# An attention-and-MLP kernel on one core: seven pairs instead of six on the seven-product path in the second group of tokens

## The chip, the core and the metric

The kernel runs on one core of a Trainium2 chip, as one launch. The metric is device time in microseconds, from one execution's start to its end. Before the change the median of three runs is 631.63 us (631.11 to 635.12).

TensorE (PE in the profile) multiplies matrices, with its weight loads shown apart as PEld. VectorE (DVE), ScalarE (ACT) and GpSimd (POOL) work elementwise. SyncE (SP) issues most of the transfers; ACT's queue issues some too.

## The reference

```
scores = scale * q @ k.T                      # 4 batches, 8 heads, 768 tokens, head size 64
keep   = is_global | is_local                 # 8 global keys, 96 local ones
scores = where(keep, scores + bias, -1e9)     # bias = -slope[head] * distance
a      = softmax(scores)
x      = (a @ v) as 3072 tokens x 512
h      = x @ w_in                             # 512 x 2048
out    = maximum(0.01 * h, h) @ w_out         # 2048 x 512
```

The weights come as float64, the rest as float32. The kernel keeps the accuracy by splitting every factor of the MLP into a high part and a low remainder and adding three products for each: high by high, low by high, high by low.

## The kernel before

The 3072 tokens go through as eleven groups: two of 384 tokens, then nine of 256. Attention is worked out one event ahead of the MLP that needs it: `late_event(t)` multiplies the attention weights of event t-2 with v (L360) and the queries and keys of event t (L218) into one PSUM tile `ps_av`, of which there is a single buffer; then come the bias and the row minima on DVE (L232), four exponentials on ACT (L245), the reciprocals (L266, L267) and four scalings on ACT (L274). `turn` transposes 32x32 blocks on DVE (L292) and sends the result through DRAM and back (`via` L256, then four `pt_d` L258), for use two events later.

The change is in the nine groups of 256 tokens. They are one loop over 72 **slots** (L902), eight for each group; slots 0 to 7 are the first group, 8 to 15 the second, 16 to 23 the third. A slot s handles one **pair** p of hidden blocks (256 of the 2048 hidden columns):

- `hidden_pair(s)` (L556): 24 matmuls of 128x256 on PE into `ps_h` (even slots) or `ps_p` (odd slots), one buffer each. The second half of their weights comes from `ring`, two buffers that are filled by transfers from DRAM (L544), issued in ACT's queue two slots ahead.
- `gates(s)`: ACT copies the sums out of PSUM (L567); DVE applies the gate (L569), and on the seven-product path four more sums of activation blocks (L572); ACT rounds to the high part `gh` (L578); DVE takes the remainder `gl` (L581).
- `products(s-2)` (L612): the second matmuls of the pair of two slots before, into banks that collect a whole group (`ps_m`, `ps_q`).

So PE's order in a slot is: an event of attention if one falls there, `hidden_pair(s)`, `products(s-2)`. This order is written out and fixed. Each engine runs its own instructions strictly in order. On DVE and ACT the order within this loop is decided when the program is built, by a scheduler; it may put an instruction well ahead of the slot in whose `gates` call it was written.

A pair goes one of two ways in `products`. The plain way is 12 matmuls of 128x512. The seven-product way forms a 2x2 block product with seven block products instead of eight: 21 matmuls of 128x256 (for pair 7, which comes first, two of them are 128x512). It needs `gates` to make the four sums of activation blocks, so `gh` and `gl` are 896 wide rather than 512, and it needs four **sums of weight blocks** for each pair, (p, 0) to (p, 3), which are made once and stay. Each, in `prepare` (L720), is three additions on DVE (L592) into one of two work buffers `wk`, a rounding on ACT (L737) and one subtraction on DVE (L592). Sums 0, 1 and 2 go to the tiles `h7`/`l7` to `h1`/`l1`; sum 3 goes over a block of the weights `wout` itself. So (p, 3) waits until the last plain pair p has been multiplied.

`SEVEN` (L33) says how many pairs of each group take the seven-product way: 0 in the first group, 6 in the second, 7 in the other seven groups. `order_of` (L526) puts the plain pairs first and the others after them from 7 downward. `sums_at` (L898 to L901) says in which slot's `gates` call each weight sum is written.

After a group's last products, `results` copies the banks out: `part<-ps_m` on ACT (L700), and, after a group of plain pairs alone, `part<-ps_q` on DVE (L702). These banks are written again two slots into the next group: the first group's last products run in slot 9, its banks are copied out, and slot 10 begins with `products(8)` in the same banks.

Of the kernel before, what the change touches and what calls it, by code (L numbers as in the profile page):

```python
# [29 lines left out]
CHUNKS = [3] * 2 + [2] * 9  # L30
STD = 2
PAIR = 2
SEVEN = [0, 6] + [7] * 7  # L33
RING = 2
EDGE = 8
LEAD_CONV = 7
# [17 lines left out]
def fast_path(ctx, tc, qp, kp, vp, wi, wo, nvec, convert, nmall, out, B, H, S):  # L54
# [11 lines left out]
    NP = NF // 2  # L66
# [59 lines left out]
    def pin(ins):  # L126

        if pinned[0]:
            tc.keep_in_program_order(ins)
# [396 lines left out]
    def order_of(c):  # L526

        n = SEVEN[c - STD]
        return list(range(NP - n)) + list(range(NP - 1, NP - 1 - n, -1))
# [57 lines left out]
    def fast(c, p):  # L587

        return p >= NP - SEVEN[c - STD]

# [105 lines left out]
    def results(c):  # L696
# [3 lines left out]
        pin(nc.scalar.copy(out=rows[0], in_=bank[3]))  # L700
        if not SEVEN[c - STD]:
            pin(nc.vector.tensor_copy(out=rows[1], in_=bank[4]))  # L702
# [66 lines left out]
    for j in range(len(order)):  # L769
# [117 lines left out]
        if j == LEFT + NF:  # L887
            early.close()
            for name, n in (("pt", 2), ("t", 2)):
# [6 lines left out]
    bank.append(ps_s.tile([P, 2 * GT], F32, tag="ps_q", name="ps_q"))  # L896
    three = [(p, n) for p in (7, 6, 5, 4) for n in range(3)]
    sums_at = {2 + n: three[2 * n:2 * n + 2] for n in range(6)}  # L898
    sums_at.update({NP: [(3, 0), (3, 1)], NP + 1: [(6, 3)], NP + 2: [(7, 3), (3, 2)], NP + 3: [(5, 3), (2, 0)],
                    NP + 4: [(4, 3), (2, 1)], NP + 5: [(3, 3), (2, 2)], NP + 6: [(2, 3)]})  # L900
    sums_at.update({2 * NP + 4 + n: [(1, n)] for n in range(4)})  # L901
    for s in range(NS):  # L902
        pinned[0] = s == 0
        for t in ev_pair.get(s, ()):
# [280 lines left out]
def tile_kernel(tc, a, out, B, H, S):  # L1185
    nc = tc.nc
    NF, _, NK, _ = a["wi"].shape
    DM = a["wo"].shape[3]
    NB = S // P
    with tc.tile_pool(name="keep", bufs=1) as keep, tc.tile_pool(name="xs", bufs=1, space=bass.MemoryType.DRAM) as dram:  # L1190
        nvec, convert = read_counts(tc, keep, a["ngl"])
        nmall = keep.tile([P, B * NB * H], F32, name="nmall")
        flag = fast_path(tc, a["qp"], a["kp"], a["vp"], a["wi"], a["wo"], nvec, convert, nmall, out, B, H, S)
        with tc.If(flag == 0):
            xs = dram.tile([B, S // 256, P, NK, 256], F32, name="xs")
            general_attention(tc, a["qt"], a["kt"], a["vt"], nvec, xs, B, H, S)
            general_ffn(tc, a["wi"], a["wo"], xs, out)
# [50 lines left out]
```

## Time and profile before

| What | Value |
|---|---|
| median of three runs | 631.63 us |
| the profiled execution | 631.47 us, of which its span 629.6 us |
| around the span | 1.9 us |
| PE busy | 607.6 us (97%) |
| DVE busy | 458.2 us (73%) |
| ACT busy | 345.9 us (55%) |
| mean granted TensorE clock | 0.996 |

The page gives the share of each engine over the whole span and in 40 slices. The chain of work that ended last is followed back from the last instruction to whatever released it. The timeline lists an engine's instructions with start, duration and, in brackets, how long the engine stood idle before and what ended the wait. The windows view gives the busy time of every engine in chosen stretches.

In this execution the second group's slots lie as follows on PE (start of the attention event or, without one, of `hidden_pair`): slot 8 at 237.25, slot 9 at 244.41, slot 10 at 251.58, slot 11 at 257.07, slot 12 at 264.02, slot 13 at 269.47, slot 14 at 276.06, slot 15 at 281.36 and slot 16 at 286.48 us. Attention events fall into slots 8, 9, 11, 13, 16, 17, 19 and 21.

### The profile page before, as it was taken

To read this page: it belongs to the slowest core of one execution; us is meant where nothing else is said; L and a number is where in the kernel's file an instruction comes from. 1 tells how busy PE (TensorE), PEld (TensorE's weight loads), DVE (VectorE), ACT (ScalarE), POOL (GpSimd) and SP (SyncE) were. 2 spreads that over 40 slices of the span, in tenths; PEclk is the share of its full clock that TensorE was granted. 3 is DMA by queue.
4 is the path that set the end of the run, shared out by engine and by line. 5 is a ranking of instruction groups with operands and counts; after the bars stand their busy time and mean duration, and the time that the engine had idled before them with its cause. 6 is when DMAs were issued, how large, how long until landed. Compare 5 with 4: busy or idle time off the path is not lost.

```text
span 629.6 us, 16801 instructions
## 1 busy us (share of the span) xinstructions
PE 607.6 (97%) x6555; PEld 561.6 (89%) x6555; DVE 458.2 (73%) x1312; ACT 345.9 (55%) x901; POOL 68.3 (11%) x118
## 2 busy tenths in 40 slices
PE   5689999999999999999999999999999999999996
PEld 4578899988888898999999999999999999999996
DVE  6989879995456997966975765766766765845654
ACT  6987755554435556556556655654655665532321
POOL 3212200000101001111011101101100100110000
PEclk9899999999999999999999999999999999999999
DMA  8886545623447755865765775855875774733411
GB/s 272 306 295 212 194 144 191 201 101 120 152 158 231 252 180 172 248 201 189 240 226 170 261 224 173 253 181 160 266 238 159 247 223 153 231 104 101 135 68 40
DMA packets 63336, 120.72 MB, mean 192 GB/s; under 512 B 8976, under 2 KB 28432, under 8 KB 63248
## 3 DMA queue, kind: packets, MB, share of 16 engines
q1 hardware_dynamic: 52880, 82.34, 40.8%
q10 hardware_dynamic: 10368, 37.23, 17.9%
q8 instruction: 53, 0.87, 0.6%
q14 instruction: 35, 0.29, 0.2%
HBM read 96.21 MB, written 23.33 MB: 190 GB/s over the span
## 4 chain that ended last, share of the span: by engine, by line
PE 85%; DVE 7%; DMA 3%; ACT 2%; issue 1%; SPq 1%; DVEq 0%; ACTq 0%
PE ps_m L612 22%; PE ps_p L556 16%; PE ps_h L556 15%; PE ps_h L472 9%; PE ps_q L612 6%; PE ps_av L360 5%; PE ps_av L218 4%; PE ps_o L1180 3%; PE ps_o L1181 3%; PE ps_o L1182 3%; DMA via<-pr 1%; DMA pt_d<-via 1%; ACT pr L245 1%; DVE w L949 1%; DVE pr L232 1%
## 5 line engine op out<-in xcount | busy, mean ns | idle before, releaser
L578 ACT CAST gh<-t 128x896 fp32r<-128x896 f32 (+1 forms) x73 | 62.5, 858 | 100.9 <-DVE t L572 56.7
L581 DVE TENSOR_TENSOR gl<-t,gh 128x896 fp32r<-128x896 f32 (+1 forms) x73 | 71.5, 980 | 49.7 <-ACT gh L578 49.7
L245 ACT ACTIVATE pr<-pr,nmall 128x192 f32<-128x192 f32 (+1 forms) x192 | 83.3, 436 | 24.0 <-DVE nmall L232 23.4
L612 PE MATMUL ps_m<-wout,gh 128*128 128x256 f32 (+1 forms) x398 | 85.8, 297 | 0.0
L569 DVE SCALAR_TENSOR_TENSOR t<-t 128x512 f32<-128x512 f32 x72 | 49.6, 689 | 31.3 <-ACT t L567 30.2
L50 POOL TENSOR_SCALAR xh<-x 128x256 fp32r<-128x256 f32 x36 | 22.6, 627 | 432.9 <-ACT x L366 352.5
L612 PEld LDWEIGHTS ps_m<-wout,gh 128*128 128x128 f32 x398 | 61.6, 188 | 1.5
L472 PE MATMUL ps_h<-xh,win 128*128 128x384 f32 x224 | 62.6, 340 | 0.1
L612 PE MATMUL ps_m<-wout,gl 128*128 128x256 f32 (+1 forms) x199 | 59.2, 297 | 0.0
L556 PE MATMUL ps_p<-xh,win 128*128 128x256 f32 x288 | 58.2, 287 | 0.0
L556 PE MATMUL ps_h<-xh,win 128*128 128x256 f32 x288 | 56.8, 282 | 0.0
L572 DVE TENSOR_TENSOR t<-t 128x128 f32<-128x128 f32 x220 | 53.9, 284 | 2.8
L556 PE MATMUL ps_h<-xh,ring 128*128 128x256 f32 x288 | 55.7, 278 | 0.0
L556 PE MATMUL ps_p<-xh,ring 128*128 128x256 f32 x288 | 55.1, 277 | 0.0
L556 PEld LDWEIGHTS ps_p<-xh,win 128*128 128x128 f32 x288 | 46.3, 188 | 6.0 <-issue 5.0
L232 DVE CUSTOM_DVE_ANT_0 pr<-ps_av,nbw 128x192 f32<-128x192 f32 x136 | 40.3, 352 | 12.0 <-ACT x L366 10.1
L556 PEld LDWEIGHTS ps_h<-xh,win 128*128 128x128 f32 x288 | 46.5, 188 | 2.4 <-issue 2.2
L612 PE MATMUL ps_m<-h,gh 128*128 128x256 f32 (+1 forms) x165 | 47.7, 289 | 0.0
L556 PEld LDWEIGHTS ps_h<-xh,ring 128*128 128x128 f32 x288 | 46.4, 189 | 0.0
L556 PEld LDWEIGHTS ps_p<-xh,ring 128*128 128x128 f32 x288 | 46.1, 188 | 0.0
L612 PE MATMUL ps_m<-h,gl 128*128 128x256 f32 x165 | 45.8, 278 | 0.0
L612 PE MATMUL ps_m<-l,gh 128*128 128x256 f32 x165 | 45.8, 278 | 0.0
(154 smaller groups left out, 1566.0 us busy)
## 6 DMA issues: line engine op xcount, KB each, us to landing
ring<-wd ACTq DMA_DIRECT2D x70, 512.0 KB, 3.6
via<-pr SPq DMA_DIRECT2D x30, 384.0 KB, 3.2
pt_d<-via SPq DMA_DIRECT2D x120, 96.0 KB, 3.2
vr<-in_vp_dram SPq DMA_DIRECT2D x40, 256.0 KB, 3.5
kr<-in_kp_dram SPq DMA_DIRECT2D x39, 256.0 KB, 4.2
wst<-in_wi_dram SPq DMA_DIRECT2D x16, 512.0 KB, 4.4
wst<-in_wo_dram SPq DMA_DIRECT2D x16, 512.0 KB, 4.1
qs<-in_qp_dram SPq DMA_DIRECT2D x24, 256.0 KB, 4.8
```

Source lines behind the costliest of these rows:

```text
L50: return eng.tensor_scalar(out=dst, in0=src, scalar1=1.0, scalar2=1.0, op0=ALU.mult, op1=ALU.mult)
L218: tc.keep_in_program_order(nc.tensor.matmul(own(u, av[qf, j, a * KW:(a + 1) * KW]), lhsT=q[rows, a, qf], rhs=keys(rows, a, f), start=True, ...
L232: pin(nc.vector.tensor_tensor_reduce(out=head(u, pr, a, j), in0=own(u, ps[:, j, a * KW:(a + 1) * KW]), in1=nb, scale=-0.125, scalar=3.0e38 ...
L245: pin(nc.scalar.activation(out=p, in_=p, func=AF.Exp, scale=-1.0, bias=nm[:, 2 * a + j:2 * a + j + 1], accum_out=sm[:, 2 * a + j:2 * a + j ...
L360: tc.keep_in_program_order(nc.tensor.matmul(av[out, a, cols], lhsT=v[rows, t, j, :], rhs=near(rows, j, t, fs), start=(n == 0), stop=(n == ...
L472: tc.keep_in_program_order(nc.tensor.matmul(ps, lhsT=win[f][:, y, k], rhs=xt[c][x][:, k, :ct], start=(k + i == 0), stop=(k == NK - 1 and i ...
L556: tc.keep_in_program_order(nc.tensor.matmul(o, lhsT=w[:, y, k], rhs=x[:, k, :], start=(k + i == 0), stop=(k == NK - 1 and i == 2)))
L569: pin(nc.vector.scalar_tensor_tensor(out=g, in0=g, scalar=0.01, in1=g, op0=ALU.mult, op1=ALU.max))
L572: pin(nc.vector.tensor_tensor(out=t[:, o], in0=t[:, x], in1=t[:, y], op=op))
L578: pin(nc.scalar.copy(out=gh[:, i - a0:j - a0], in_=t[:, i:j]))
L581: pin(nc.vector.tensor_tensor(out=gl[:, i - a0:j - a0], in0=t[:, i:j], in1=gh[:, i - a0:j - a0].bitcast(F32), op=ALU.subtract))
L612: tc.keep_in_program_order(nc.tensor.matmul(to, lhsT=x[:, a], rhs=y, start=first and n == 0, stop=last and n == 2))
```

## The change

```diff
-SEVEN = [0, 6] + [7] * 7
+SEVEN = [0] + [7] * 8
...
     three = [(p, n) for p in (7, 6, 5, 4) for n in range(3)]
     sums_at = {2 + n: three[2 * n:2 * n + 2] for n in range(6)}
-    sums_at.update({NP: [(3, 0), (3, 1)], NP + 1: [(6, 3)], NP + 2: [(7, 3), (3, 2)], NP + 3: [(5, 3), (2, 0)],
-                    NP + 4: [(4, 3), (2, 1)], NP + 5: [(3, 3), (2, 2)], NP + 6: [(2, 3)]})
-    sums_at.update({2 * NP + 4 + n: [(1, n)] for n in range(4)})
+    sums_at.update({NP: [(3, 0), (3, 1)], NP + 1: [(6, 3), (5, 3)], NP + 2: [(7, 3), (3, 2)], NP + 3: [(4, 3), (2, 0)],
+                    NP + 4: [(3, 3), (2, 1)], NP + 5: [(2, 2), (1, 0)], NP + 6: [(2, 3), (1, 1)], NP + 7: [(1, 2)],
+                    2 * NP: [(1, 3)]})
```

`NP` is 8. In the second group pair 1 now takes the seven-product way, and the group's order of pairs becomes 0, 7, 6, 5, 4, 3, 2, 1 instead of 0, 1, 7, 6, 5, 4, 3, 2. So slot 9 is pair 7 on the seven-product way, where it was pair 1 on the plain way. The four sums of pair 1, which were written in slots 20 to 23, are written in slots 13 to 16. No sum is added or dropped over the whole kernel.

The order of instructions changes at three places.

**PE, the products of slot 9, which run in slot 11.** Before, the first rows of the plain pair:

```order
L612 MATMUL ps_m_2676<-wout_85,gh_3553 128x512 x2
L612 MATMUL ps_m_2676<-wout_85,gl_3554 128x512
L612 MATMUL ps_q_2677<-wout_85,gh_3553 128x512 x2
L612 MATMUL ps_q_2677<-wout_85,gl_3554 128x512
L612 MATMUL ps_m_2676<-wout_85,gh_3553 128x512 x2
```

Now, the first rows of pair 7's seven products:

```order
L612 MATMUL ps_m_2674<-h7_2926,gh_3557 128x512
L612 MATMUL ps_m_2674<-l7_2927,gh_3557 128x256
L612 MATMUL ps_m_2674<-h7_2926,gl_3558 128x256
L612 MATMUL ps_m_2674<-wout_85,gh_3557 128x256 x2
L612 MATMUL ps_m_2674<-wout_85,gl_3558 128x256
```

Twelve matmuls of 128x512 have become 21 narrower ones.

**DVE, from the gate of slot 7 to the bias of slot 8's attention event.** L569 is the gate, L581 the remainder `gl`, L592 a step of a weight sum, L232 the bias, L266 and L267 the reciprocals. Before:

```order
L569 SCALAR_TENSOR_TENSOR t_3323<-t_3323 128x512
L581 TENSOR_TENSOR gl_3329<-t_3323,gh_3328 128x512
L232 ISA pr_3387,nmall_65<-ps_av_3354,nbw_156 128x2x96
L232 ISA nmall_65 128x1
...
L266 TENSOR_SCALAR rs_3397<-sm_3392 128x4
L267 RECIPROCAL rs_3397<-rs_3397 128x4
L569 SCALAR_TENSOR_TENSOR t_3433<-t_3433 128x512
```

Now:

```order
L569 SCALAR_TENSOR_TENSOR t_3323<-t_3323 128x512
L592 TENSOR_TENSOR wout_85<-wk_2784,wout_85 128x256
L592 TENSOR_TENSOR wk_2784<-wout_85,h3_3441 128x256
L592 TENSOR_TENSOR wk_2784<-wk_2784,wout_85 128x256
L581 TENSOR_TENSOR gl_3329<-t_3323,gh_3328 128x512
L592 TENSOR_TENSOR wk_2784<-wk_2784,l3_3442 128x256
L592 TENSOR_TENSOR l3_3442<-wk_2784,h3_3441 128x256
L592 TENSOR_TENSOR wk_2784<-wout_85 128x256
L592 TENSOR_TENSOR wk_2784<-wk_2784,wout_85 128x256 x2
L232 ISA pr_3387,nmall_65<-ps_av_3354,nbw_156 128x2x96
```

From the gate of slot 7 to the gate of slot 9 DVE had 8 instructions of L592 and now has 24; up to the gate of slot 7 the two orders hold the same number, with (5, 3) in the place of (7, 3).

**ACT, from the copy of slot 9's event out of PSUM to the copy-out of the first group's bank.** Before:

```order
L366 COPY x_3499<-ps_av_3474 128x256
L245 ACTIVATE pr_3505,sm_3510<-pr_3505,nmall_65 128x2x96 x4
L567 COPY t_3548<-ps_p_2673 128x512
L544 DMA ring_3550<-wd_122 128x1024
L737 CAST h2_3740<-wk_2784 128x256
L274 ACTIVATE pr_3505<-pr_3505,rs_3515 128x2x96 x4
L737 CAST wout_85<-wk_2784 128x256
L700 COPY part_3582<-ps_m_2676 128x512
L578 CAST gh_3553<-t_3548 128x512
```

Now:

```order
L737 CAST h1_3946<-wk_2784 128x256
L366 COPY x_3499<-ps_av_3474 128x256
L245 ACTIVATE pr_3505,sm_3510<-pr_3505,nmall_65 128x2x96 x4
L567 COPY t_3548<-ps_p_2673 128x512
L544 DMA ring_3550<-wd_122 128x1024
L737 CAST h1_3946<-wk_2784 128x256
L274 ACTIVATE pr_3505<-pr_3505,rs_3515 128x2x96 x4
L737 CAST wout_85<-wk_2784 128x256
L700 COPY part_3591<-ps_m_2676 128x512
L578 CAST gh_3557<-t_3548 128x896
```

The rows stand in the same order; the roundings between them belong to other weight sums (`h1` in the place of `h3` and `h2`), and `gh` of slot 9 is 896 wide.

## The prediction

> **What bounds the kernel now.** I read the page first, then the chain of waits in the second group, then the busy time slot by slot, then the timelines of DVE and ACT.
>
> ```profile
> PE 607.6 (97%) x6555; PEld 561.6 (89%) x6555; DVE 458.2 (73%) x1312; ACT 345.9 (55%) x901; POOL 68.3 (11%) x118
> PE 85%; DVE 7%; DMA 3%; ACT 2%; issue 1%; SPq 1%; DVEq 0%; ACTq 0%
> ```
>
> TensorE sets the time. In the changed group it does so without a break:
>
> ```profile
> 248.83 0.69 PE ps_m L612 x3
> ...
> 250.89 0.69 PE ps_q L612 x3
> 251.58 2.75 PE ps_h L556 x24
> 254.32 0.69 PE ps_m L612 x3
> ...
> 273.68 1.70 PE ps_m L612 x15
> 275.72 0.34 PE ps_m L612 x3
> 276.06 2.83 PE ps_h L556 x24
> ```
>
> Each piece starts where the one before ends. So nothing that other engines do here costs time as long as it comes before PE wants it. How near that is, the stretches from slot 8 to 11 show (columns: PE, PEld, DVE, ACT, POOL busy):
>
> ```profile
> 237.25:244.41 7.16, 7.16 (x88) 6.09 (x91) 4.32 (x16) 4.96 (x17) 1.37 (x2) 1.00 0.69 203
> 244.41:251.58 7.17, 7.17 (x87) 6.38 (x87) 6.51 (x22) 4.29 (x16) 1.15 (x2) 1.00 0.40 120
> 251.58:257.07 5.49, 5.49 (x40) 4.72 (x42) 5.42 (x13) 3.21 (x8) 0.00 (x0) 1.00 1.09 319
> 257.07:264.02 6.95, 6.95 (x87) 6.29 (x87) 6.88 (x25) 3.92 (x14) 2.06 (x2) 1.00 0.67 228
> ```
>
> DVE is full in slots 9 to 11 (6.51 of 7.17, 5.42 of 5.49, 6.88 of 6.95 us). Only slot 8 has room, 2.84 us. There the change puts its extra sums.
>
> **The products: a gain of 0.37 us.** In the chain above a plain pair takes 251.58 - 248.83 = 2.75 us on PE (12 matmuls of 128x512), a seven-product pair 276.06 - 273.68 = 2.38 us. One pair changes sides, so PE needs 0.37 us less. Pair 7's two wide matmuls stay two; they move from slot 10 to slot 9.
>
> **The sums of weight blocks: DVE comes late.** Up to the gate of slot 7 both orders hold as much on DVE. From there to the gate of slot 9 there are 24 steps of weight sums (L592) in the place of 8. The rows of before:
>
> ```profile
> 236.42 0.42 DVE L592 TENSOR_TENSOR wk<-wout,h 128x256 f32<-128x256 f32 x1
> 236.75 0.41 DVE L592 TENSOR_TENSOR wk<-wk,l 128x256 f32<-128x256 f32 x1
> ...
> 237.88 0.68 DVE L569 SCALAR_TENSOR_TENSOR t<-t 128x512 f32<-128x512 f32 x1
> 239.30 0.69 DVE L581 TENSOR_TENSOR gl<-t,gh 128x512 fp32r<-128x512 f32 x1 [0.74 <-ACT gh L578]
> 239.91 0.35 DVE L232 CUSTOM_DVE_ANT_0 pr<-ps_av,nbw 128x192 f32<-128x192 f32 x1
> ...
> 242.20 0.17 DVE L266 TENSOR_SCALAR rs<-sm 128x4 f32<-128x4 f32 x1 [1.10 <-ACT pr L245]
> 242.67 0.69 DVE L569 SCALAR_TENSOR_TENSOR t<-t 128x512 f32<-128x512 f32 x1
> 244.21 0.98 DVE L292 STREAM_TRANSPOSE pr<-pr 128x768 f32<-128x768 f32 x1 [0.84 <-ACT pr L274]
> 245.11 0.38 DVE L592 TENSOR_TENSOR wout<-wk,wout 128x256 fp32r<-128x256 f32 x1
> ...
> 246.01 0.42 DVE L592 TENSOR_TENSOR wk<-wout,h 128x256 f32<-128x256 f32 x1
> 246.47 0.42 DVE L592 TENSOR_TENSOR wk<-wk,wout 128x256 f32<-128x256 f32 x1
> ...
> 247.82 0.42 DVE L592 TENSOR_TENSOR l<-wk,h 128x256 fp32r<-128x256 f32 x1 [0.47 <-ACT h L737]
> 248.17 0.35 DVE L232 CUSTOM_DVE_ANT_0 pr<-ps_av,nbw 128x192 f32<-128x192 f32 x1
> ...
> 250.93 0.69 DVE L569 SCALAR_TENSOR_TENSOR t<-t 128x512 f32<-128x512 f32 x1
> ```
>
> From gate 7 (237.88) to gate 9 (250.93) DVE now takes 13.05 us, of which 0.74 + 1.10 + 0.84 + 0.47 = 3.15 us are waits. What will it take with 24 steps? A step costs, start to start, 0.33 us where the next instruction doesn't need its result (236.42 to 236.75; I take 0.34) and 0.46 where it does (246.01 to 246.47). By the new order about 7 of the 24 are followed by one that needs them: 7 x 0.46 + 17 x 0.34 = 9.0 us. The rest, start to start: two `gl` 1.2 (239.30 to 239.91), two gates of the same size 1.2, two biases 2.2 (from 239.91 to where the wait before 242.20 begins, 241.10, less the last row's overlap), one transpose 0.9 (244.21 to 245.11), two pairs of reciprocals 0.9 (242.20 to 242.67). One wait stays: the subtraction of sum (3, 2) stands directly behind its last addition and waits for ACT's rounding, 0.5 us, as at 247.82. Sum: 16.0 us. So gate 9 runs at 253.9 in the place of 250.93, **3.0 us late**. Nearly all the waits of before are filled, and the rest of the added work has nowhere to go.
>
> **Who waits for that.** Behind gate 8 and the bias of slot 9's event comes ACT, which has little work of its own here but takes it in order:
>
> ```profile
> 250.33 0.56 ACT L567 COPY t<-ps_p 128x512 f32<-128x512 f32 x1
> ...
> 251.11 1.49 ACT L274 ACTIVATE pr<-pr,rs 128x192 f32<-128x192 f32 x4
> 252.50 0.39 ACT L737 CAST wout<-wk 128x256 fp32r<-128x256 f32 x1
> 252.80 0.58 ACT L700 COPY part<-ps_m 128x512 f32<-128x512 f32 x1
> ```
>
> L700 empties the first group's bank `ps_m`. It stands behind the four scalings, which need slot 9's reciprocals from DVE, and these need the exponentials, and those the bias (248.17), all 3.0 us late. L700 then ends at 253.38 + 3.0 = 256.4 us. PE wants that bank at:
>
> ```profile
> 254.16 0.62 PE L612 MATMUL ps_m<-wout,gh 128*128 128x512 f32 x2
> ```
>
> Before, L700 was 0.78 us early. Now PE stands for 3.0 - 0.78 = **2.2 us** at the start of slot 10's products. The other bank (`ps_q`, L702 on DVE) is wanted 0.69 us after that and comes free at about 256.2, so it adds nothing.
>
> Sum: 631.47 + 2.2 - 0.37 = **633.3 us**. The profiled execution lies 0.16 us below the median of the runs (631.63); I leave that.
>
> The price of a step is the unknown. With every step at 0.33 the stretch is 1.1 us shorter, the lateness 1.9, the wait 1.1: 632.2. With every step at 0.46 it is 2.0 us longer, the wait 4.2: 635.3. I take the mixture, since the order shows which kind each is.
>
> [...]
>
> **What is hidden.** The 16 steps that leave slots 18 to 20 free DVE there, where PE doesn't wait before either: no gain. The added ACT work of slot 9 (`gh` of 896 instead of 512) and its four DVE additions come behind L700 and L702. By then the wait has moved PE back by 2.2 us, so DVE is only 0.8 us worse placed than before. It gets this back in slots 10 and 11, which have lost the sums that were done early. Slots 12 and 13 then hold the last sums (1, 2) and (1, 3), seven more steps ahead of slot 13's gate, 2.6 us, of which a wait for ACT like the 1.06 us below takes up a part: 1.5 us remain. The remainder of slot 13 is the next that could be late:
>
> ```profile
> 280.00 1.09 DVE L581 TENSOR_TENSOR gl<-t,gh 128x896 fp32r<-128x896 f32 x1 [1.06 <-ACT gh L578]
> ...
> 284.10 1.70 PE ps_m L612 x15
> ```
>
> It ends at 281.09 and PE wants it at 284.10, 3.0 us later. With DVE 1.5 us worse placed relative to PE, 1.5 us are left.
>
> The transposed block of slot 8's event is 3.0 us later too, and is wanted in slot 11, which begins at 257.07:
>
> ```profile
> L258 SPq DMA_DIRECT2D pt_d<-via x4: 319/426/436, 249.7 to 251.0; - x4
> DMA to landing us min/median/max: 2.9/4.4/4.5
> ```
>
> The last of the four issues (251.0) lands by 255.5. Three us later that is 258.5, and slot 11 then begins at 259.3: hidden by 0.8 us, because PE has waited already. If L700 weren't late, this would be the wait, with 1.4 us.
>
> **Rivals.**
>
> *Not slower: DVE takes the sums into its waits.* Place: the same stretch. PE waits only if DVE is over 0.78 us late at L700. For it: 3.15 us of waits are in that stretch, and PE waited for nobody before. Against it: the 24 steps would have to cost 0.28 us each, less than the 0.33 of any pair of rows here. It would also need the transfer above to be 1.4 us quicker. Time: 631.47 - 0.37 = 631.1 us.
>
> *A second wait.* The lateness doesn't heal: if the seven steps before slot 13's gate cost 0.46 each (3.2 us in the place of 2.6) and three of them wait 0.5 us for ACT's roundings, DVE is 1.5 + 0.6 + 1.5 = 3.6 us behind where 3.0 are left, so PE waits 0.6 us in slot 15, and as much again one slot on: 633.3 + 1.2 = 634.5 us. Against it stands slot 15, where DVE has 3.92 us of work to PE's 5.12 and so gains over a microsecond:
>
> ```profile
> 281.36:286.48 5.12, 5.12 (x50) 4.99 (x51) 3.92 (x11) 1.53 (x2) 0.00 (x0) 1.00 0.51 170
> ```
>
> *The clock.* The granted clock fell once where PE stood much:
>
> ```profile
> 10.00:25.00 15.00, 9.85 (x288) 7.82 (x288) 14.62 (x54) 13.69 (x47) 6.25 (x12) 0.89 0.82 278
> 199.00:206.30 7.30, 6.86 (x48) 5.84 (x46) 5.03 (x19) 5.55 (x17) 0.35 (x1) 1.00 0.87 296
> ```
>
> Of 15 us 5.15 were idle, and the mean 0.89 loses 1.65 us. If a wait of 2.2 us does that too: 633.3 + 1.65 = 635.0 us. Against it: a break of 0.44 us left the clock at 1.00. [...]
>
> **How the numbers follow.** My forecast, 633.3 us with its own range of 632.2 to 635.3, has 0.60; not slower (631.1) 0.17; a second wait (634.5) 0.16; the clock (635.0) 0.06; anything else 0.01. The range 630.9 to 635.8 us takes in the first rival and the two later ones. One per cent, about what a measurement of this kernel can tell from no change, is 6.3 us. None of the cases reaches it: faster by over 1% would need 625.3, slower 637.9. I give 0.01 and 0.04, the latter for two or three causes together; 0.95 for within 1%.
>
> **What would show it.** In the profile of the changed kernel: in PE's timeline an idle time of about 2 us before the first `ps_m` of slot 10, released by ACT's `part` L700; gate 9 of DVE near 253.9; the products of slot 9 in 2.4 us; no L592 on DVE in slots 18 to 20, and PE's pieces there as long as before. Wrong would be: no wait at L700 (then a step is cheaper than its rows), a wait on `pt_d` in slot 11 in its place, a wait of PE on `gl` in slots 12 to 17, or a change of time without any new wait of PE.

## The result

| | before | after |
|---|---|---|
| median | 632.26 us (6 runs) | 638.15 us (637.08 to 640.07, 6 runs) |
| the profiled execution | 631.47 us, span 629.6 | 637.08 us, span 635.3 |
| PE busy | 607.6 us | 609.8 us |
| mean granted clock | 0.996 | 0.988 |

The change costs 0.83% (ratio 1.0083, 1.0066 to 1.0101), 5.9 us. The forecast was 633.3 and the range ended at 635.8. So the sign was right and the size too small: 638.15 lies 4.9 us above the forecast. Of these, 0.8 us is that the median of before was 632.26 here and not the 631.47 from which the forecast started; the change itself was forecast at 1.8 us.

The page of after begins like that of before, and hardly shows it:

```profile
PE 609.8 (96%) x6564; PEld 564.1 (89%) x6564; DVE 461.6 (73%) x1316; ACT 346.2 (54%) x901; POOL 67.8 (11%) x118
PE 79%; DVE 12%; ACT 3%; DMA 3%; issue 2%; SPq 0%; ACTq 0%; DVEq 0%
```

The chain that ended last has 12% of DVE in the place of 7%, and 79% of PE in the place of 85%. The timeline of PE between slots 8 and 12 says where: two waits, where before had none.

```profile
245.38 0.90 PE L360 MATMUL ps_av<-pt_d,vr 64*64 64x128 f32 x26 [1.18 <-ACT pr L245]
258.68 1.22 PE L612 MATMUL ps_m<-wout,gh 128*128 128x512 f32 x2 [3.21 <-ACT part L700]
```

The second is the wait that was forecast, at the instruction that was forecast, but 3.2 us and not 2.2. The first, in slot 9, was not forecast. And a third loss follows, in the chain behind the second wait:

```profile
258.68 1.65 PE ps_m L612 x3
260.33 1.28 PE ps_q L612 x3
261.61 0.89 PE ps_m L612 x3
262.50 0.70 PE ps_q L612 x3
```

Each of these took 0.69 us before. The windows view names the reason (columns: PE, PEld, DVE, ACT, POOL busy, then the granted clock, the DMA share and GB/s):

```profile
252.57:258.06 5.49, 2.91 (x25) 2.71 (x23) 5.03 (x21) 4.24 (x16) 0.00 (x0) 1.00 0.86 214
258.06:269.94 11.88, 11.26 (x105) 9.82 (x106) 10.97 (x33) 6.42 (x19) 1.52 (x2) 0.86 0.73 223
```

11.88 us at a mean clock of 0.86 lose 1.7 us. In finer windows the clock is 1.00 up to 258.25, 0.50 from 258.5 to 261.75 and 0.70 in the quarter of a microsecond after that: it fell just as the wait ended. DVE is busy almost throughout, 5.03 of 5.49 and 10.97 of 11.88 us. (The mean clocks in the table differ by more than this loss. The rest lies in the first 30 us: between 10 and 30 us after lost some 4.8 us of clock and before 1.7, and slot 8 began no later for it.)

Take the start of each slot's `hidden_pair` and count from slot 8's, in both profiles. Slot 9 then begins 1.38 us later than before, and slot 11 another 4.97 us later (3.2 of wait, the rest clock). Up to slot 13 the shorter products win back 0.38 us, and from there to slot 20 the distance stays at 5.97 us within 0.1. The spans differ by 5.7 us.

DVE's rows in after, from the gate of slot 7 (the first L569) to that of slot 9 (the last):

```profile
238.46 0.68 DVE L569 SCALAR_TENSOR_TENSOR t<-t 128x512 f32<-128x512 f32 x1
...
241.82 0.42 DVE L592 TENSOR_TENSOR l<-wk,h 128x256 fp32r<-128x256 f32 x1 [0.47 <-ACT h L737]
242.28 0.54 DVE L592 TENSOR_TENSOR wk<-wout 128x256 f32<-128x256 f32 x1
242.86 1.31 DVE L592 TENSOR_TENSOR wk<-wk,wout 128x256 f32<-128x256 f32 x2
...
244.92 0.35 DVE L232 CUSTOM_DVE_ANT_0 pr<-ps_av,nbw 128x192 f32<-128x192 f32 x1
...
247.00 0.66 DVE L569 SCALAR_TENSOR_TENSOR t<-t 128x512 f32<-128x512 f32 x1
...
251.01 0.62 DVE L592 TENSOR_TENSOR wk<-wout,h 128x256 f32<-128x256 f32 x1
251.55 0.96 DVE L592 TENSOR_TENSOR l<-wk,h 128x256 fp32r<-128x256 f32 x1
...
256.19 0.69 DVE L569 SCALAR_TENSOR_TENSOR t<-t 128x512 f32<-128x512 f32 x1
```

Gate to gate 17.73 us, where before took 13.05 and the forecast was 16.0. The 24 steps take 10.8 us from start to start, not 9.0. Some of them are long, 0.62 or 0.96 us instead of 0.42, and beside these stand rows of GpSimd, which splits the attended values there:

```profile
242.15 0.40 POOL L50 TENSOR_SCALAR xh<-x 128x256 fp32r<-128x256 f32 x1 [16.81 <-ACT x L366]
242.64 0.79 POOL L397 TENSOR_TENSOR xl<-x,xh 128x256 fp32r<-128x256 f32 x1
250.95 0.40 POOL L50 TENSOR_SCALAR xh<-x 128x256 fp32r<-128x256 f32 x1 [7.52 <-ACT x L366]
251.44 0.79 POOL L397 TENSOR_TENSOR xl<-x,xh 128x256 fp32r<-128x256 f32 x1
```

In before the same two splits fell elsewhere:

```profile
239.63 0.63 POOL L50 TENSOR_SCALAR xh<-x 128x256 fp32r<-128x256 f32 x1 [14.86 <-ACT x L366]
...
248.64 0.74 POOL L397 TENSOR_TENSOR xl<-x,xh 128x256 fp32r<-128x256 f32 x1
```

There DVE was doing the biases (L232, 0.35 us each with or without GpSimd beside them), which read only one operand from SBUF and one from PSUM. In after the biases come later, for the added steps stand ahead of them, and the splits now fall on those steps. (The first split begins later too: ACT's copy L366, which starts it, stands behind two more roundings of weight sums, the second of which waits 1.53 us for DVE.)

### The profile page after: what moved, and what is told of

Read it like the earlier page. It is cut to its first block, busy times and chain, and to the rows that moved or that the text cites. A ratio compares the mean times of both kernels' runs of the same rounds, so it can differ in the third digit from the quotient of the medians.

```text
span 635.3 us, 16823 instructions
## 1 busy us (share of the span) xinstructions
PE 609.8 (96%) x6564; PEld 564.1 (89%) x6564; DVE 461.6 (73%) x1316; ACT 346.2 (54%) x901; POOL 67.8 (11%) x118
## 4 chain that ended last, share of the span: by engine, by line
PE 79%; DVE 12%; ACT 3%; DMA 3%; issue 2%; SPq 0%; ACTq 0%; DVEq 0%
PE ps_m L612 20%; PE ps_p L556 14%; PE ps_h L556 13%; PE ps_h L472 10%; PE ps_q L612 5%; PE ps_av L360 4%; PE ps_av L218 3%; DVE wk L592 3%; PE ps_o L1181 3%; PE ps_o L1180 3%; PE ps_o L1182 3%; ACT pr L245 2%; DVE pr L232 1%; DMA via<-pr 1%; DVE gl L581 1%
## 5 line engine op out<-in xcount | busy, mean ns | idle before, releaser
L581 DVE TENSOR_TENSOR gl<-t,gh 128x896 fp32r<-128x896 f32 (+1 forms) x73 | 72.0, 987 | 50.6 <-ACT gh L578 50.6
L245 ACT ACTIVATE pr<-pr,nmall 128x192 f32<-128x192 f32 (+1 forms) x192 | 83.3, 435 | 26.4 <-DVE nmall L232 26.4
L569 DVE SCALAR_TENSOR_TENSOR t<-t 128x512 f32<-128x512 f32 x72 | 49.7, 690 | 33.5 <-ACT t L567 32.2
L232 DVE CUSTOM_DVE_ANT_0 pr<-ps_av,nbw 128x192 f32<-128x192 f32 x136 | 40.3, 352 | 11.4 <-ACT x L366 11.4
```

The lines of the kernel that those rows point to most:

```text
L232: pin(nc.vector.tensor_tensor_reduce(out=head(u, pr, a, j), in0=own(u, ps[:, j, a * KW:(a + 1) * KW]), in1=nb, scale=-0.125, scalar=3.0e38 ...
L245: pin(nc.scalar.activation(out=p, in_=p, func=AF.Exp, scale=-1.0, bias=nm[:, 2 * a + j:2 * a + j + 1], accum_out=sm[:, 2 * a + j:2 * a + j ...
L569: pin(nc.vector.scalar_tensor_tensor(out=g, in0=g, scalar=0.01, in1=g, op0=ALU.mult, op1=ALU.max))
L581: pin(nc.vector.tensor_tensor(out=gl[:, i - a0:j - a0], in0=t[:, i:j], in1=gh[:, i - a0:j - a0].bitcast(F32), op=ALU.subtract))
```

## The experiments

The theory after the result: the early sums alone cost the time, by four things one behind the other. More steps than counted wait for the one before; GpSimd's split lengthens some; TensorE so waits in slots 9 and 10; and behind the longer wait the clock falls to 0.50. The rivals: the seventh pair is the cost; the copy-out L700 is only an unlucky place in ACT's queue; DVE lacks the time altogether, so that any remedy brings its wait back elsewhere. Each run below has one kept trace; what is read from it holds for that execution.

All ratios are to the kernel before on the same chip, in rounds of their own.

**The change once more.** 

> The change again, beside the others on one chip and with a second profile. Theory (the losses are those of the order, not of one execution): the wait at the copy-out in slot 10 within 1 us of the 3.2 us of the first profile, a wait of about 1 us on the attention bank in slot 9, the lowered clock in slot 10, and 636.5 to 638.5 us. Rival (part of it was that execution's own lateness of VectorE at the gate of slot 7, 0.8 us): a wait near 2.4 us, none in slot 9, and a median nearer 636.

638.27 us, ratio 1.0104 (1.0087 to 1.0122). The waits of PE:

```profile
PE ps_m L612 <- ACT part L700: 3.2, 1, 3.2
PE ps_av L360 <- ACT pr L245: 0.9, 1, 0.9
```

The losses belong to the order. What varies from one execution to the next is the wait in slot 9: gate 7 lies 0.02 us behind the start of slot 8's `hidden_pair` in the first profile and 0.27 ahead of it in this one, and the waits are 1.18 and 0.89. The clock fell to 0.50 here too, for some 3.4 us, but only about 0.9 us after the wait had ended.

**The sums alone, six pairs.** One line is put back:

```diff
-SEVEN = [0] + [7] * 8
+SEVEN = [0, 6] + [7] * 7
```

> The new table of weight sums, with the second group's pairs as before (six on the seven-product path). My theory, as the trace after the change corrects it: VectorE gets 24 steps of weight sums between the gates of slots 7 and 9 instead of 8, is late, and TensorE waits about 1.2 us in slot 9 (for the bias to leave the attention tile) and about 3.2 us in slot 10 (for the first group's bank), then runs some 1.6 us slower at a lowered clock. All of that comes from the table, so this kernel shows the same two waits and takes 0.4 us more than the change: 638.5 us, 1.008 to 1.010 of before. Rival: the seventh pair itself (four more additions and a wider rounding in slot 9) makes VectorE late; then this kernel is within 1 us of before, 632 to 633 us.

638.96 us, ratio 1.0085 (1.0066 to 1.0104). The wait at L700 is again 3.21 us, that in slot 9 is 1.66, with gate 7 at 239.22, 0.50 behind the start of slot 8's `hidden_pair`:

```profile
246.14 0.90 PE L360 MATMUL ps_av<-pt_d,vr 64*64 64x128 f32 x26 [1.66 <-ACT pr L245]
259.45 1.22 PE L612 MATMUL ps_m<-wout,gh 128*128 128x512 f32 x2 [3.21 <-ACT part L700]
```

The seventh pair is not the cause. The clock stayed low longer here (a mean of 0.50 from 260 to 264 us and 0.70 in the 2 us after that), and slot 20 begins 7.9 us late. Not every execution lost this: one of the six took 636.15 us with a mean clock of 0.999, which leaves at most 1 us lost in the whole span.

**The seventh pair alone.** The sums go back to the slots of the kernel before, with pair 1's four in slots 14 to 16. Against the change this is:

```diff
-    sums_at.update({NP: [(3, 0), (3, 1)], NP + 1: [(6, 3), (5, 3)], NP + 2: [(7, 3), (3, 2)], NP + 3: [(4, 3), (2, 0)],
-                    NP + 4: [(3, 3), (2, 1)], NP + 5: [(2, 2), (1, 0)], NP + 6: [(2, 3), (1, 1)], NP + 7: [(1, 2)],
+    sums_at.update({NP: [(3, 0), (3, 1)], NP + 1: [(6, 3)], NP + 2: [(7, 3), (3, 2)], NP + 3: [(5, 3), (2, 0)],
+                    NP + 4: [(4, 3), (2, 1)], NP + 5: [(3, 3), (2, 2)], NP + 6: [(2, 3), (1, 0)], NP + 7: [(1, 1), (1, 2)],
```

> Seven pairs in the second group, but the sums of weight blocks in the slots of the kernel before as far as they go (pair 1's four sums follow in slots 14 to 16): up to the gate of slot 9 VectorE's order is that of the kernel before, 8 weight-sum steps and not 24. Theory (the early sums cost the time, the seventh pair is free): no wait of TensorE on the copy-out of the bank in slot 10, clock kept there, and the seven-product gain of 0.37 us stays: 0.2 to 0.5 us under the kernel before, unless the sums that now crowd slots 10 to 13 make a new wait; with one, up to 1 us above it. Rival (the seventh pair itself is what comes too early, its four additions, its wider rounding and remainder in slot 9): 2 us or more above the kernel before, with waits of TensorE in slots 10 to 12.

632.08 us, ratio 0.9991 (0.9972 to 1.0010). PE waits for nobody, and DVE's gates 7 and 9 are 13.06 us apart:

```profile
237.98 0.69 DVE L569 SCALAR_TENSOR_TENSOR t<-t 128x512 f32<-128x512 f32 x1
...
251.04 0.69 DVE L569 SCALAR_TENSOR_TENSOR t<-t 128x512 f32<-128x512 f32 x1
```

From slot 13 to 18 everything lies 0.37 us sooner than before. That is the gain of the seventh pair, and too small for the interval.

> Seven pairs with the earlier kernel's slots for the sums, again, to narrow the ratio to the kernel before (0.9991, 0.9972 to 1.001). Theory: no wait of TensorE from slot 8 to slot 20, products of the seventh pair 0.3 to 0.4 us shorter, ratio 0.999 to 1.000. Rival: the first profile was lucky, and in this one the sums in slots 10 to 13 make TensorE wait in slots 11 to 14; ratio 1.001 or more.

633.01 us, ratio 1.0009 (0.9985 to 1.0033): between theory and rival. In this profile the gain is used up. DVE copies out the other bank behind three of the seventh pair's additions, and PE's first `ps_q` of slot 10 starts at 254.96, 0.27 us after it could:

```profile
254.23 0.68 DVE L702 COPY part<-ps_q 128x512 f32<-128x512 f32 x1
```

So the pair is worth nothing that can be measured, in either direction. The early sums are the whole loss, as far as these intervals tell.

**Without GpSimd's split in slots 8 and 9.** ACT rounds and DVE subtracts straight from PSUM:

```diff
-        keep_x(t - 2, av)
+        direct = t in (ev_pair[NP] + ev_pair[NP + 1])
+        if direct:
+            high, low = parts(t - 2, av)
+            high()
+        else:
+            keep_x(t - 2, av)
...
+            if direct:
+                low()
...
-        split_x(t - 2)
+        if not direct:
+            split_x(t - 2)
```

> The change, with the attention results of the two events in slots 8 and 9 split into high part and remainder by ScalarE and VectorE from PSUM, not by GpSimd from a copy. ScalarE's work stays the same (one pass of 0.37 us each), VectorE gets 0.34 us more for each event. Theory: several steps of weight sums take 0.6 to 0.96 us in the trace of the change just when GpSimd splits, where 0.42 is usual; without GpSimd all take 0.42, VectorE gains some 1.2 us and pays 0.7, and TensorE's waits in slots 9 and 10 shrink by about 0.5 us together: 637.5 us. If GpSimd has nothing to do with the long steps, they stay long and the time rises by 0.7 us to about 638.8.

635.5 us, ratio 1.0038 (1.0024 to 1.0052): 2 us better than expected. The groups of steps in the stretch between the gates (minimum, median and longest in ns), first of after, then of this kernel, where the line of a step is L600 and that of the copy-out L708:

```profile
L592 DVE TENSOR_TENSOR wk<-wk,wout x10: 386/424/848, 240.0 to 255.0; 128x256 f32<-128x256 f32 x10
L592 DVE TENSOR_TENSOR l<-wk,h x4: 420/422/959, 241.8 to 251.5; 128x256 fp32r<-128x256 f32 x4
```

```profile
L600 DVE TENSOR_TENSOR wk<-wk,wout x9: 419/422/428, 240.5 to 255.2; 128x256 f32<-128x256 f32 x9
L600 DVE TENSOR_TENSOR l<-wk,h x4: 415/416/424, 242.4 to 254.2; 128x256 fp32r<-128x256 f32 x4
```

No step is long any more: the long ones were GpSimd's doing. The stretch shrinks to 16.6 us although DVE now makes the subtractions as well, and PE's waits to 0.57 and 2.14 us:

```profile
258.10 0.72 PE L620 MATMUL ps_m<-wout,gh 128*128 128x512 f32 x2 [2.14 <-ACT part L708]
```

This is near the forecast wait of 2.2 us, but by luck: gate 9 is later than forecast (3.9 us relative to slot 8, not 3.0), and PE had itself lost 0.9 us by slot 10. The clock fell to 0.50 behind this wait. That did not happen in every execution either: two of the six have a mean clock of 0.999, which leaves at most 1 us lost.

In after the step at 251.55 meets L397 of GpSimd, which ends at 252.23, and ends 0.28 us after it. The other three long steps of after, which begin at 242.28, 242.86 and 251.01, also end 0.27 or 0.28 us after the GpSimd row that they meet.

The same edit to the kernel before, where DVE has waits to spare:

> The kernel before, with GpSimd's split of the attended values in slots 8 and 9 done by ScalarE and VectorE instead. Theory (GpSimd's reads cost time only where weight-sum steps with two inputs from SBUF run beside them and TensorE waits for VectorE): within 0.4 us of the kernel before, since TensorE waits for nobody there. Rival (the split is dear anywhere, through TensorE's later operands): 1 us or more faster.

631.99 us, ratio 0.9992 (0.9973 to 1.0012). So it costs nothing measurable where it doesn't fall on steps that PE waits for.

**Keeping TensorE busy.** 28 matmuls more at the start of slot 10, into the bank that `hidden_pair` overwrites:

```diff
+        if s == 10:
+            w, x = win[2 * p], xt[c][0]
+            for _ in range(28):
+                tc.keep_in_program_order(nc.tensor.matmul(ps[:, :GT], lhsT=w[:, 0, 0], rhs=x[:, 0, :], start=True, stop=True))
```

> The change, with 28 more matmuls of 128x256 at the start of slot 10, whose results are overwritten by the next matmul into the same place. They take about 3.2 us, as long as TensorE waits for the first group's bank at the end of that slot, so TensorE works through the time in which it stood. Theory that the wait lowers the clock: the wait is gone from the profile, nothing else moves, the clock stays at 1.00 in slot 10 and its products take 2.8 us instead of 4.45; 636.5 us, 1.6 us below the change. Rival, that the lowered clock has another cause or costs nothing: 638 us as the change.

637.53 us, ratio 1.0081 (1.0064 to 1.0098): nearer the rival's, and no gain over the change that the intervals show. In the trace the clock is kept:

```profile
254.50:258.30 3.80, 3.80 (x36) 3.79 (x34) 3.34 (x10) 3.68 (x12) 0.00 (x0) 1.00 0.86 238
258.30:262.20 3.90, 3.90 (x58) 3.10 (x60) 3.36 (x8) 1.50 (x3) 0.00 (x0) 1.00 0.63 243
```

and slot 11 begins 1.8 us sooner than in after. But up to slot 20 1.2 us of that are given back, partly by a wait on DVE in slot 15 that after doesn't have:

```profile
288.68 0.38 PE L616 MATMUL ps_m<-h,gl 128*128 128x256 f32 x1 [0.38 <-DVE gl L585]
```

So in the trace the clock's loss is real, and part of it had hidden DVE's lateness; what it is worth in the median isn't shown. Half the fill, 14 matmuls:

> The change with 14 matmuls of 128x256 more at the start of slot 10 instead of 28 (about 1.5 us of the wait of 3.2 filled). Left over is one wait of about 1.7 us at the copy-out. [...]

637.61 us, ratio 1.0093 (1.0075 to 1.0110), as with 28. Behind the wait of 1.66 us that is left the clock stays at 1.00:

```profile
258.72 0.72 PE L616 MATMUL ps_m<-wout,gh 128*128 128x512 f32 x2 [1.66 <-ACT part L704]
```

```profile
258.30:262.20 3.90, 3.48 (x32) 2.70 (x36) 3.83 (x9) 1.86 (x4) 0.00 (x0) 1.00 0.80 247
```

The times don't show what that is worth: 637.61 us fits both the 637.53 us of 28 matmuls and the 638 of the change.

**Both together,** no split by GpSimd and 20 matmuls of fill:

> The change without GpSimd's split in slots 8 and 9, and with 20 matmuls of 128x256 more at the start of slot 10 (about 2.2 us, into the bank that the hidden pair then overwrites), so that TensorE doesn't stand still while VectorE is late. The fill takes the place of the wait of 2.14 us and saves only the halved clock behind it. Theory (what the prediction left out is GpSimd's reads, the clock and the wait in slot 9; with the first two gone its sum is nearly right): full clock in slot 10, no wait at the copy-out, 1.8 us less than without the fill, so 633.4 to 634.2 us. Rival (VectorE is late behind slot 10 as well, and what the clock no longer takes comes back as waits): 635 us or more.

636.71 us, ratio 1.0074 (1.0060 to 1.0088). The trace shows what the theory wanted: no wait at the copy-out, full clock, slot 11 1.7 us sooner than without the fill, 0.7 us of it given back up to slot 20. The times don't: they spread from 635.18 (the profiled execution) to 637.5, and the ratio is above that without the fill (1.0038). What the slower executions wait for isn't shown; that stays open. The rival's number is the one that was measured.

**The sums later,** with seven pairs:

```diff
-    sums_at.update({NP: [(3, 0), (3, 1)], NP + 1: [(6, 3), (5, 3)], NP + 2: [(7, 3), (3, 2)], NP + 3: [(4, 3), (2, 0)],
-                    NP + 4: [(3, 3), (2, 1)], NP + 5: [(2, 2), (1, 0)], NP + 6: [(2, 3), (1, 1)], NP + 7: [(1, 2)],
-                    2 * NP: [(1, 3)]})
+    sums_at.update({NP: [(3, 0)], NP + 1: [(6, 3), (3, 1)], NP + 2: [(7, 3)], NP + 3: [(5, 3), (3, 2)],
+                    NP + 4: [(4, 3), (2, 0)], NP + 5: [(3, 3), (2, 1)], NP + 6: [(2, 2), (1, 0)], NP + 7: [(2, 3), (1, 2)],
+                    2 * NP: [(1, 1), (1, 3)]})
```

> Seven pairs as in the change, but each weight sum in the latest slots that its product allows: 10 steps instead of 24 stand on VectorE between the gates of slots 7 and 9. My theory: no wait in slot 9, at most 0.5 us in slot 10, no lowered clock there; 632 to 633.5 us, with up to 1.5 us more if the sums that now crowd slots 10 to 13 make VectorE late there. Rival, the seventh pair itself: the waits stay and the time is above 636 us.

635.74 us, ratio 1.0045 (1.0030 to 1.0059): 2 to 4 us worse than the 632 to 633.5 of the theory, and just under the 636 of the rival. Only 10 steps stand between gates 7 and 9, but 6 of these come ahead of slot 8's bias, and two of them wait half a microsecond each for ACT's roundings. GpSimd's split falls among steps again: between 250 and 252 us it takes 1.06 us, and four instructions fill 1.93 us of DVE. The stretch takes 15.5 us, and the waits of PE are smaller but not gone:

```profile
257.28 0.74 PE L612 MATMUL ps_m<-wout,gh 128*128 128x512 f32 x2 [1.81 <-ACT part L700]
258.62 1.22 PE L612 MATMUL ps_q<-wout,gh 128*128 128x512 f32 x2 [0.38 <-DVE part L702]
```

```profile
258.30:262.20 3.90, 3.58 (x9) 2.81 (x9) 3.90 (x11) 1.25 (x3) 0.00 (x0) 0.56 1.00 346
```

Here the clock fell behind waits of 1.81 and 0.38 us that lie close together. The number of steps is not all that counts: where they stand so early they also bring waits.

**The copy-out moved away from its queue.** Slot 9's products go ahead of its attention event:

```diff
+        early = s == NP + 1
+        if early:
+            out_pair(s - 2)
         for t in ev_pair.get(s, ()):
             late_event(t)
         hidden_pair(s)
...
-        if s >= 2:
+        if s >= 2 and not early:
             out_pair(s - 2)
```

> The change, with slot 9's products (the last of the first group) ahead of slot 9's attention event on TensorE instead of behind its hidden pair. So the first group's banks are ready 7 us earlier and their copy-out no longer stands behind slot 9's exponentials and scalings; the event of slot 9 and its hidden pair come 2.8 us later on TensorE. Theory (TensorE waits at the copy-out only, everything else has room): no wait in slots 9 and 10, full clock: 632 to 633 us. Rival (VectorE's work is the limit and the copy-out only the first place where it shows): the wait comes back on something else in slots 10 to 13 (the remainder of a pair, the transposed block, the attention bank), and the time is 634 to 636.

635.14 us, ratio 1.0037 (1.0016 to 1.0059): the rival's. Slots 9 and 10 are free of waits. In slot 11 they come back:

```profile
261.02 0.38 PE L556 MATMUL ps_p<-xh,ring 128*128 128x256 f32 x1 [1.42 <-DMA ring<-wd]
263.59 0.39 PE L612 MATMUL ps_m<-h,gl 128*128 128x256 f32 x1 [0.54 <-DVE gl L581]
```

The transfer into the ring was issued on ACT's queue at 256.35, behind exponentials that waited 0.73 us for DVE. So L700 is only the first place where DVE's lateness shows, though the loss is smaller when it shows later.

**Both remedies against it,** the earlier table and no split by GpSimd:

> Seven pairs with the earlier kernel's slots for the sums, and slots 8 and 9 without GpSimd's split: the two remedies together. Theory: 0 to 0.5 us under the kernel with the sums alone moved back, so 0.3 to 0.8 us under the kernel before, as little of the sums is left beside GpSimd's split. Rival (the rounding taken over by ScalarE and the subtraction by VectorE delay the copy-out in slot 10): a wait of 0.3 to 1 us there and a time above the kernel before.

632.79 us, ratio 1.0001 (0.9981 to 1.0021). No wait, as the theory had it, but not its gain of 0.3 to 0.8 us: none that can be told from zero. Nothing here beats the kernel before.

## Why the prediction was too small

**Right:** the bound, the place, and the chain behind it. PE waits for L700 in slot 10, since DVE is late at the gate of slot 9. The product gain is 0.37 us (measured 0.37 with the seventh pair alone, 0.38 in after). No step of a weight sum is left in slots 18 to 20, and nothing is gained there. (Seven rows of L592 do stand in slot 18; they combine the group's results, as in before, so "no L592" was the wrong sign to look for.) The wait for ACT's rounding is there with 0.47 (taken as 0.5), and PE waits for nothing from slot 11 to 20, `pt_d` and the remainders among it.

**Failed: "7 x 0.46 + 17 x 0.34 = 9.0 us".** Measured 10.8. About 1.3 us is GpSimd's split, a resource that the step didn't ask about: its rows in before lay beside the biases. Some 0.5 us is steps that wait for the one before, at 0.46: about 11 of them and not 7. The rest of the stretch was right within 0.1 us (7.0 forecast, 6.9 measured). The lateness relative to PE was 5.5 us, not 3.0: 1.7 from this, and 0.8 from an offset that DVE already had at gate 7. Less the 1.38 us that PE lost in slot 9 and the 0.78 that L700 was early, this leaves 3.3 us, and PE waited 3.2.

**Failed: no offset at gate 7.** The prediction put this term at nothing, since both orders hold the same number of steps up to there. In the five profiles with the sums of before in slots 7 to 9, gate 7 lies 0.41 to 1.04 us ahead of slot 8's `hidden_pair`; in the eight with the table of the change it lies between 0.57 us ahead and 0.50 behind. So it varies from one execution to the next and tends to be later with the change. Why is not shown.

**Failed: one consumer left out.** The step "who waits for that" followed gate 8 and the bias of slot 9's event, and forgot the bias of slot 8's own. That one reads the single `ps_av`, which PE wants again in slot 9. Before, its last row ended at about 241.1 and PE came at 244.41, so 3.3 us were there:

```profile
240.74 0.35 DVE L232 CUSTOM_DVE_ANT_0 pr<-ps_av,nbw 128x192 f32<-128x192 f32 x1
```

In after it ends at 245.27, and PE starts 0.11 us later. (The profile names ACT's L245, which does not read `ps_av`; the DVE row tells more. In the second profile of the change and in that with 14 matmuls PE starts 0.12 and 0.11 us after the bias; in that without the split and with 20 matmuls of fill, where DVE subtracts from `ps_av` behind the bias, 0.10 us after that.) Cost 0.9 to 1.4 us in the two profiles of the change.

**Failed: the clock as a rival of its own with 0.06.** It was weighed at a wait of 2.2 us and with steps at their middle price. But dearer steps make the wait longer, and in the prediction's own rows the clock had fallen where PE stood much (0.89 with 5.15 of 15 us idle). So steps at 0.46 *and* the clock was a case too: 635.3 + 1.65 = 637.0 us from the same rows. The range reached to each of the two and not to both. The break of 0.44 us that was set against it shows nothing of a wait of 2.2 us: the clock fell to 0.50 behind waits of 3.2 and 2.14 us here, and behind 1.81 with 0.38, while it stayed at 1.00 behind 1.66 us, and behind 1.42 with 0.54 in the kernel with the products first.

But in these profiles the length of a wait does not decide it. One of 2.13 us stands in the first 10 us of before, and the clock (the third number from the end of the second view) stayed at 1.00 until 16 us:

```profile
8.27 1.13 PE L218 MATMUL ps_sc<-kr,qs 64*64 64x128 f32 x16 [2.13 <-DMA kr<-in_kp_dram]
```

```profile
0.00:10.00 10.00, 4.90 (x46) 3.83 (x50) 5.45 (x35) 5.20 (x19) 2.39 (x15) 1.00 0.76 255
```

In after 1.76 and 1.38 us stand close together at the same place, and there the clock was 0.50 from about 9.3 to 12.7 us. So the clock belonged among the rivals, as the prediction had it. That it fell behind a wait of 3.2 us is measured; a limit in microseconds is not.

**The sum as it was,** in the profiled execution: 1.4 in slot 9 + 3.2 at L700 + 1.75 by the clock - 0.38 = 5.97 us, against 2.2 - 0.37 = 1.83.

**The rivals:** "not slower" is refuted by all profiles of this order of sums. "A second wait" on `gl` didn't come in after, where PE lost 6 us and so gave DVE time; it came in the slot named for it, 15, with 0.38 us, when the clock's loss was filled.

## What to carry to other kernels

Work that goes into the waits of a full engine makes everything behind it late by what doesn't fit (here DVE's gate 9 by 5.5 us relative to PE); walk through every consumer in the stretch, the nearest first, and ask of each how early it was. A row's duration holds for the neighbours that it had (0.42 us here, and 0.96 beside GpSimd's subtraction): when work moves in time, look which other engine's rows it now stands beside. And where one unknown feeds another, as here the price of a step fed the wait of 3.2 us, behind which the clock was 0.50, the range has to hold both at their ends together.

## What the runs showed of the hardware

- In the profile of the change a weight-sum step with both inputs from SBUF takes 0.42 us alone and up to 0.96 beside GpSimd's 0.79 us subtraction; the four long ones end 0.27 or 0.28 us after the GpSimd row that they meet. A bias with one input from PSUM takes 0.35 us beside a GpSimd row (in before) as without one.
- Behind waits of TensorE of 2.14 and 3.2 us in slot 10 the granted clock was 0.50 for some 3.4 us (1.7 to 1.8 us lost), in one profile for 6.9 us; behind one of 1.66 us it stayed at 1.00. At the kernel's start it also stayed at 1.00 behind 2.13 us in before. So the length alone does not tell.
- With matmuls whose result nobody reads in the place of a wait the clock stayed at 1.00 in all three such profiles, but with 28 of them the gain shrank from 1.8 us at once to 0.65 us nine slots on, and the median shows none.
